# Sliding-window attention and gated layer on one core: where a step's loads, odd value copies and small norm stand in the queues

## The chip, the cores and the metric

The kernel runs on 1 core of one Trainium2 chip. The metric is the device time of one execution in microseconds (us). Four executions of the kernel before took 284.91 to 287.67 us, median 287.3 us. The profiled one took 287.19 us; its span, from the first to the last instruction, is 285.5 us, and its granted TensorE clock is 0.998.

## The reference

Windowed attention on 8 batches, 8 heads, 576 positions, head size 64, and then a two-layer network on the 4608 tokens of 512 features:

```python
scores = (1.0 / np.sqrt(D)) * np.matmul(q, k.transpose(0, 1, 3, 2))
mask = np.abs(pos[:, None] - pos[None, :]) <= 32
attn = softmax(np.where(mask, scores, -1e9))          # rows sum to 1 (+1e-09)
x = np.matmul(attn, v).transpose(0, 2, 1, 3).reshape(B * S, H * D)
h = x @ w_in                                          # 512 -> 2048
g = h * (1.0 / (1.0 + np.exp(-1.702 * h)))
return (g @ w_out).astype(np.float32)                 # 2048 -> 512
```

## The kernel before

Tokens are cut into 36 units of 128 and 18 pairs of 256. The order of work on every engine is written out by hand. `head` and `window(4)` do the first pairs; `steady(w)` runs for w = 5 to 17 and is a software pipeline over three pairs: attention of pair w (units 2w and 2w+1), first layer of pair t = w-1 and second layer of pair o = w-2; `last` and `close` empty the pipeline. Both layers use seven block products in place of eight (`seven` and `product`, on VectorE sums `x_sums`, `g_sums`, and weight sums made once).

The attention of a step: `scores` needs kT and qT (transposed keys and queries in a ring of 1536 tokens); ScalarE takes the exponential, VectorE multiplies the band mask (`band`); `values_two` multiplies with the values, of which two copies are kept: `ve` (8 units, as loaded) and `vo` (the same shifted by 64 tokens, the "odd value copies", made by `odd_pair` with DMAs on SyncE's queue). Heads 0 to 6 of both units go to one pair of banks, head 7 to bank b0; `norm_two(w, 7)` (lines 387, 388) divides head 7, the "small norm", and `norm_two(w, 0)` (lines 390, 391) divides the rest and issues `x_T`: two DMA transposes that make xT of pair w (line 404, SyncE's queue). The first layer of pair w begins in step w+1 and needs that xT; its x sums are line 728.

`seven(t, 1, 0)` writes into bank b0, so TensorE can't start it until the small norm has read it.

Transfers of a step, in the order of their queues before the change:
- GpSimd: `gate` (line 784), a copy of one element of xT[w-1] that can't run until that xT has landed, and then `loads(w)`: two loads into `ve` (units 2w+6, 2w+7), two of k rows and two of q rows (units 2w+8, 2w+9); at a batch boundary one of them is cut in two.
- SyncE: `odd_pair(2w+2)` (lines 190 to 195, two or three copies), xT of pair w (line 404, two transposes), `feed(w)` (line 172, two kT and two qT transposes of units 2w+6 and 2w+7, whose rows `loads(w-1)` brought), and two output stores (line 516). `feed` runs up to w = 14.

Each engine issues its list strictly in order, so an item of SyncE's list that waits holds those behind it. The outputs go through three `o_sb` buffers: in the program, `result(o, 22)` of a step (line 505) waits for the first store of the step before.

In `head`, the q rows of the third tile of 512 tokens are transposed on TensorE into bank "o" four times and copied out by ScalarE; the first second-layer product of `window(4)` (line 436) takes the same bank "o".

Of the kernel before, what the change touches and what calls it, by code (L numbers as in the profile page):

```python
# [27 lines left out]
class _Kernel:  # L28
# [504 lines left out]
    def head(self):  # L533

        nc, dve, act, pool = self.nc, self.nc.vector, self.nc.scalar, self.nc.gpsimd
# [131 lines left out]

        def rows(hp):
            self.rows_T("k", 2, hp, "t", dve)
            self.rows_T("q", 2, hp, "o", act)  # L670

        self.seven(2, 1)
        self.move("side", "main", dve)
# [7 lines left out]
        self.move("k2", "main", act)  # L681
        self.layer1(2, 1, "b")
        rows(0)
        self.x_T(6, "b")
        self.seven(2, 7)
        self.move("k7", "side", act)
        self.seven(2, 5)
        rows(1)
        self.move("22", "main", dve, "k7")
        self.layer1(2, 2, "b")  # L690
        self.gelu(2, "22", 1, 1)
        rows(2)
        self.layer1(2, 3, "b")
        self.seven(2, 4)
# [85 lines left out]
    def steady(self, w):  # L780

        dve, act = self.nc.vector, self.nc.scalar
        a, b, t, o = 2 * w, 2 * w + 1, w - 1, w - 2
        self.nc.gpsimd.tensor_copy(self.gate[0:1], self.xT[t][0:1, 0, 255:256])  # L784
        self.loads(w)
        self.product(o, 1, "o")
        self.scores(a, which=0)
        self.scores(b, which=1)
        if w + 1 < self.NW:
            self.odd_pair(2 * w + 2)  # L790
        self.keep(o, 1, dve)
        self.g_sums(o, 0, (0,))
        self.product(o, 2, "t")
        self.g_sums(o, 0, (1,))
        self.g_sums(o, None, (2,))
        self.product(o, 6)
        self.result(o, 11)
        self.product(o, 5, "t")
        self.keep(o, 6, dve)
        self.band(a)  # L800
        self.seven(t, 1, 1)
        self.product(o, 7)
        self.band(b)
        self.x_sums(t, (0,))
        self.move("side", "main", dve, half=1)
        self.values_two(w)
        self.gelu_table()
        self.x_sums(t, (1,))
        self.keep(o, 7, dve)
        self.seven(t, 2, 1)  # L810
        self.x_sums(t, (2,))
        self.norm_two(w, 7)
        self.seven(t, 6, 1)
        self.gelu(t, "side", 0, 0, 1)
        self.norm_two(w, 0)
        self.seven(t, 1, 0)
        self.move("k2", "main", act, half=1)
        self.product(o, 4)
        self.move("side", "main", dve, half=0)
        self.seven(t, 7, 1)  # L820
        self.x_sums(t, (3,))
        if w == 5:
            self.w_in_sums(0, (2,))
        self.seven(t, 5, 1)
        self.move("k7", "side", act, half=1)
        self.seven(t, 2, 0)
        self.move("22", "main", dve, "k7", 1)
        self.feed(w)
        self.seven(t, 6, 0)
        self.gelu(t, "side", 0, 0, 0)  # L830
        self.seven(t, 4, 1)
        self.g_sums(o, None, (3,))
        self.move("k2", "main", act, half=0)
        self.seven(t, 7, 0)
        self.result(o, 22)
        self.gelu(t, "22", 1, 1, 1)
        self.seven(t, 3, 1)
        self.move("21", "side", dve, "k2", 1)
        self.move("k7", "side", act, half=0)
        self.seven(t, 5, 0)  # L840
        self.gelu(t, "21", 1, 0, 1)
        self.product(o, 3)
        self.move("22", "main", dve, "k7", 0)
        self.result(o, 21, act)
        self.gelu(t, "main", 0, 1, 1)
        self.seven(t, 4, 0)
        self.result(o, 12)
        self.gelu(t, "22", 1, 1, 0)
        self.seven(t, 3, 0)
        self.move("21", "side", dve, "k2", 0)  # L850
        self.gelu(t, "main", 0, 1, 0)
        self.g_sums(t, 1, (0,))
        self.gelu(t, "21", 1, 0, 0)
        self.g_sums(t, 1, (1,))
# [88 lines left out]
    def window(self, w):  # L943

        dve, act = self.nc.vector, self.nc.scalar
        a, b = 2 * w, 2 * w + 1

        def run(lst, n=1):
            for _ in range(min(n, len(lst))):
                lst.pop(0)()  # L950

        l2 = [(lambda u=u, i=i: self.layer2(u, i, "oh"[u % 2], (dve, act)[u % 2])) for u in (4, 5) for i in range(4)]
        run(l2)
        self.scores(7, which=0)
        self.scores(a, which=1)
        run(l2, 2)
        self.band(7)
        self.scores(b, which=0)
        run(l2)
        self.band(a)  # L960
        self.values(7, "th")
        self.gelu_table()
        self.band(b)
        self.norm(7)
        run(l2, 2)
        self.values(a, which=1)
        self.values(b, which=0)
        run(l2)
        self.x_T(7, "t", act)
        self.norm(a)  # L970
        self.x_T(a)
        self.norm(b)
        self.x_T(b)
        run(l2)
        self.loads(w)
        self.odd_pair(10)
        self.w_sums(2, 0)
        self.chain(w - 1, ("b", "a", "b", "a"), lambda: self.feed(w),
                   lambda: [self.w_sums(n, 1) for n in (0, 1, 2, 3)])
        self.g_sums(w - 1, 1, (0, 1))  # L980

    def close(self):
# [91 lines left out]
```

## Time and profile before

| What | Value |
|---|---|
| Profiled execution: its time, its span | 287.19 us, 285.5 us |
| Median of 4 executions (lowest, highest) | 287.3 us (284.91, 287.67) |
| Busy share: PE, DVE, ACT, POOL | 96%, 83%, 73%, 37% |
| Chain that ended last: PE, DMA, DVE, ACT | 41%, 25%, 13%, 10% |
| DMA queue of GpSimd (loads), packets | 97232, 84.6% of 16 engines' span |
| DMA queue of SyncE, packets | 49504, 52.1% |
| xT issues of steps 5 to 17, first and last | 85.87 us, 257.85 us |

The distance between the xT issues of two steps (line 404 in the timeline of SyncE) is a step's length; the twelve distances sum to 171.98 us. The gate's start (line 784 in the timeline of POOL) tells when an xT had landed, since the gate waits for it. A busy PE is not one at its peak, as matmuls are pipelined; so a step's length says more than PE's share. DMA shares of the two queues overlap and can add up to more than 100%.

### The profile page before, as it was taken

The numbers are of one execution on the slowest core, as the hardware profiler recorded it, in microseconds if no ns is written. First come the engines' busy times: TensorE is split into PE (matmuls) and PEld (weight loads), VectorE is DVE, ScalarE is ACT, GpSimd is POOL, SyncE is SP. The second block draws the span as 40 slices with busy tenths as digits, with TensorE's granted clock in tenths as the row PEclk, the third lists the DMA queues.
The fourth block names the chain that finished last, engine by engine and source line by source line (L and its number), as shares of the span: only waits on it lengthen the run. The fifth ranks groups of instructions, "written<-read, shape, count | busy, mean of one in ns | idle before, by whom it ended". The sixth has DMA issues, their size and how long they took to land.

```text
span 285.5 us, 10594 instructions
## 1 busy us (share of the span) xinstructions
PE 274.5 (96%) x4477; PEld 233.2 (82%) x4478; DVE 236.4 (83%) x550; ACT 207.3 (73%) x343; POOL 106.1 (37%) x153
## 2 busy tenths in 40 slices
PE   7999999999999999999999999999989999999995
PEld 2668654865989798989898989898979898989994
DVE  7765567789899889898988888989878989898783
ACT  4576466695778778787887787878777878787360
POOL 8864424997170344434343453433420000000000
PEclk9999999999999999999999999999999999999999
DMA  9999999999999999999999999999999543213022
GB/s 154 188 198 205 200 183 157 175 138 120 207 149 141 131 207 169 166 157 182 137 197 118 215 136 205 161 173 176 146 109 217 137 120 88 66 49 89 27 77 74
DMA packets 147232, 42.42 MB, mean 149 GB/s; under 512 B 130416, under 2 KB 141424, under 8 KB 147184
## 3 DMA queue, kind: packets, MB, share of 16 engines
q0 software_dynamic: 97232, 18.16, 84.6%
q1 hardware_dynamic: 49504, 23.19, 52.1%
q8 instruction: 35, 0.57, 0.9%
q10 hardware_dynamic: 448, 0.39, 0.5%
q14 instruction: 13, 0.11, 0.1%
HBM read 36.96 MB, written 9.44 MB: 163 GB/s over the span
## 4 chain that ended last, share of the span: by engine, by line
PE 41%; DMA 25%; DVE 13%; ACT 10%; POOL 6%; issue 3%; SPq 1%; POOLq 0%; DVEq 0%; ACTq 0%
PE o_ps L487 16%; PE h_main L751 12%; DMA xT<-x 10%; PE h_side L751 9%; DMA w_out_sb<-in_moe_w_out_dram 5%; DMA qs<-in_q_dram 4%; ACT g L768 3%; DMA w_in_sb<-in_moe_w_in_dram 3%; ACT L310 2%; DVE h_side L123 2%; DVE xs L728 2%; DMA ve<-in_v_dram 2%; ACT p L310 2%; POOL ve L177 2%; ACT p L308 2%
## 5 line engine op out<-in xcount | busy, mean ns | idle before, releaser
L751 PEld LDWEIGHTS <-w_in_sb 128*128 128x128 f16 x960 | 59.5, 98 | 7.0 <-issue 2.4
L487 PEld LDWEIGHTS <-gs 128*128 128x128 f16 x480 | 45.3, 98 | 6.0 <-DVE gs L466 0.8
L784 POOL COPY gate<-xT 1x1 f16<-1x1 f16 x13 | 4.0, 310 | 116.0 <-DMA xT<-x 116.0
L751 PEld LDWEIGHTS <-wi_sum 128*128 128x128 f16 x720 | 43.3, 98 | 0.0
L768 ACT ACTIVATE g<-hs 128x512 f16<-128x512 f32 x60 | 37.8, 630 | 0.6 <-DVE hs L763 0.6
L177 POOL DMA_DIRECT2D ve<-in_v_dram x41 | 34.5, 857 | 9.8 <-DMA w_out_sb<-in_moe_w_out_dram 3.5
L751 PE MATMUL h_main<-xs,wi_sum 128*128 128x128 f16 x480 | 36.4, 219 | 0.0
L487 PEld LDWEIGHTS <-g 128*128 128x128 f16 x360 | 32.9, 98 | 3.8
L751 PE MATMUL h_side<-xs,w_in_sb 128*128 128x128 f16 x480 | 34.3, 219 | 0.0
L768 ACT ACTIVATE g<-h_side 128x512 f16<-128x512 f32 x30 | 17.9, 598 | 21.9 <-PE h_side L751 21.6
L763 DVE TENSOR_TENSOR hs<-h_main,hs 128x512 f32<-128x512 f32 x30 | 20.7, 691 | 12.9 <-ACT hs L123 8.4
L487 PE MATMUL o_ps<-w_out_sb,g 128*128 128x256 f16 x240 | 31.1, 273 | 0.0
L487 PE MATMUL o_ps<-w_out_sb,gs 128*128 128x256 f16 x240 | 30.9, 273 | 0.0
L123 ACT COPY hs<-h_side 128x512 f32<-128x512 f32 x30 | 17.5, 583 | 18.1 <-PE h_side L751 17.9
L487 PE MATMUL o_ps<-w_sum,gs 128*128 128x256 f16 x240 | 28.7, 273 | 0.4 <-DVE gs L466 0.4
L436 PE MATMUL o_ps<-w_out_sb,g 128*128 128x512 f16 x96 | 23.4, 380 | 0.7 <-ACT qT L123 0.7
L320 DVE TENSOR_TENSOR p<-p,mask 128x1024 bf16<-128x1024 bf16 x32 | 22.2, 699 | 2.2 <-ACT p L310 0.7
L165 POOL DMA_DIRECT2D qs<-in_q_dram x27 | 23.0, 882 | 2.1 <-DMA ks<-in_k_dram 1.6
L165 POOL DMA_DIRECT2D ks<-in_k_dram x27 | 23.0, 880 | 0.0
L424 PE MATMUL h_ps<-xT,w_in_sb 128*128 128x256 f16 x192 | 22.6, 273 | 0.0
L123 DVE COPY part<-o_ps 128x256 f32<-128x256 f32 x45 | 18.9, 421 | 4.3 <-PE o_ps L487 4.3
L763 DVE TENSOR_TENSOR hs<-h_side,hs 128x512 f32<-128x512 f32 x30 | 20.6, 687 | 1.4 <-PE h_side L751 0.9
(112 smaller groups left out, 546.0 us busy)
## 6 DMA issues: line engine op xcount, KB each, us to landing
out_dram<-o_sb SPq DMA_DIRECT2D x34, 256.0 KB, 4.2
ve<-in_v_dram POOLq DMA_DIRECT2D x31, 128.0 KB, 7.5
ks<-in_k_dram POOLq DMA_DIRECT2D x24, 128.0 KB, 8.1
qs<-in_q_dram POOLq DMA_DIRECT2D x24, 128.0 KB, 10.5
vo<-ve SPq DMA_DIRECT2D x22, 132.0 KB, 6.2
w_in_sb<-in_moe_w_in_dram POOLq DMA_DIRECT2D x4, 512.0 KB, 8.8
w_out_sb<-in_moe_w_out_dram POOLq DMA_DIRECT2D x4, 512.0 KB, 14.4
ve<-in_v_dram POOLq DMA_DIRECT2D x10, 64.0 KB, 5.9
```

Source lines behind the costliest of these rows:

```text
L123: (eng.copy if eng is self.nc.scalar else eng.tensor_copy)(out, in_)
L165: self.nc.gpsimd.dma_start(self.stage[key][off:off + m, n], src[b, :, s:s + m, :].rearrange("h s d -> s h d"))
L177: self.nc.gpsimd.dma_start(self.ve[lo + off:lo + off + n, m % NV, :, :self.D], self.v[b, :, s:s + n, :].rearrange("h s d -> s h d"))
L308: nc.scalar.activation(p[:, eo], sc[eo], AF.Exp, scale=self.scale)
L310: nc.scalar.activation(p.rearrange("k e h s -> k e (h s)"), both, AF.Exp, scale=self.scale)
L320: self.nc.vector.tensor_mul(pv, pv, msk.to_broadcast([128, 8, 2, SQ]))
L424: nc.tensor.matmul(hps[:, i, :], self.w_in_sb[:, kr, ff * 128:(ff + 1) * 128], self.xT[t][:, kr, :], start=(i == 0 and kr == 0), stop=(i = ...
L436: nc.tensor.matmul(o_ps, self.g[t][:, ff, s * 128:(s + 1) * 128], self.w_out_sb[:, ff, :], start=(ff == 0), stop=(ff == self.NFF - 1))
L487: nc.tensor.matmul(self.part[t, key], x, y, start=(first and k == 0), stop=(k == 7), skip_group_check=True)
L751: self.nc.tensor.matmul(dst[:, f], a, b, start=(n in (1, 7) and f == 0 and k == 0), stop=(f == 3 and k == 1), skip_group_check=True)
L763: self.nc.vector.tensor_add(hs[key, half], hs[src, half], hs[add, half])
L768: self.nc.scalar.activation(self.g[t][:, at:at + 4, 128 * v:128 * v + 128], self.hs[src, half], AF.Gelu_apprx_sigmoid)
```

## The change

Four edits. (1) In a steady step, `odd_pair`, the gate and `loads(w)` are put behind `norm_two(w, 0)`, and the gate reads xT[w] in place of xT[w-1]. On SyncE's queue the odd copies of a step come behind its xT; on GpSimd's queue each step's loads wait for that step's xT. (2) `x_sums(t, (2,))` stands behind the small norm on VectorE, not ahead of it. (3) The fourth q copy of the third tile uses a "b" bank. (4) The first g sum of the first steady step is made at the end of `window`.

```diff
@@ head @@
-            self.rows_T("q", 2, hp, "o", act)
+            self.rows_T("q", 2, hp, "ooob"[hp], act)
@@ steady @@
-        self.nc.gpsimd.tensor_copy(self.gate[0:1], self.xT[t][0:1, 0, 255:256])
-        self.loads(w)
         self.product(o, 1, "o")
         self.scores(a, which=0)
         self.scores(b, which=1)
-        if w + 1 < self.NW:
-            self.odd_pair(2 * w + 2)
         self.keep(o, 1, dve)
-        self.g_sums(o, 0, (0,))
+        if w > 5:
+            self.g_sums(o, 0, (0,))
         self.product(o, 2, "t")
...
         self.seven(t, 2, 1)
-        self.x_sums(t, (2,))
         self.norm_two(w, 7)
         self.seven(t, 6, 1)
+        self.x_sums(t, (2,))
         self.gelu(t, "side", 0, 0, 1)
         self.norm_two(w, 0)
+        if w + 1 < self.NW:
+            self.odd_pair(2 * w + 2)
+        self.nc.gpsimd.tensor_copy(self.gate[0:1], self.xT[w][0:1, 0, 255:256])
+        self.loads(w)
         self.seven(t, 1, 0)
@@ window @@
+        self.g_sums(w - 1, 0, (0,))
         self.g_sums(w - 1, 1, (0, 1))
```

No instruction is added or removed but for the place of these. In a steady step SyncE's list becomes: xT of pair w, `odd_pair(2w+2)`, `feed(w)`, two stores.

## The prediction

> **What bounds the kernel now.** I read the windows view first, with one window from xT issue to xT issue (a step), then the chain, the queues' timelines and the waits.
>
> ```profile
> 142.94:157.67 14.73, 14.29 (x251) 12.91 (x249) 12.57 (x29) 11.51 (x19) 5.98 (x9) 1.00 1.97 159
> 186.26:200.29 14.03, 14.02 (x251) 12.72 (x249) 12.48 (x29) 11.51 (x19) 5.14 (x8) 1.00 1.74 179
> 200.29:216.68 16.39, 15.20 (x269) 13.76 (x267) 13.21 (x30) 11.82 (x20) 4.51 (x6) 1.00 1.76 141
> 229.73:243.74 14.01, 14.00 (x251) 12.70 (x249) 12.46 (x29) 11.51 (x19) 0.18 (x1) 1.00 0.30 79
> sum 171.98, PE 168.83 PEld 153.23 DVE 151.46 ACT 137.98 POOL 50.42; mean PE 14.07 PEld 12.77 DVE 12.62 ACT 11.50 POOL 4.20
> ```
>
> Columns: window, length, busy PE, PEld, DVE, ACT, POOL, clock, DMA share, GB/s. The clock is full everywhere. The floor is 14.02 us: a late step almost without DMA (share 0.30) has it, so there the compute engines set the pace. Twelve steps at 14.02 are 168.24; the sum is 171.98, so 3.74 us of waits stand above the floor. The long steps lie where the DMA share is near 2, and the chain shows what ended last in one:
>
> ```profile
> 144.88 9.23 DMA xT<-x
> 154.21 0.29 DVE xs L728
> 155.63 0.20 DVE xs L728
> 155.95 0.30 DVE x L388
> 156.30 0.62 PE h_main L751 x8
> ```
>
> The xT landed at 154.11, 0.6 us after VectorE wanted it. Then VectorE works down to the small norm (L388), and TensorE's next product starts right behind that. The two queues of this step:
>
> ```profile
> 139.50 0.32 POOL L784 COPY gate<-xT 1x1 f16<-1x1 f16 x1 [7.74 <-DMA xT<-x]
> 143.94 1.78 POOL L165 DMA_DIRECT2D qs<-in_q_dram  x2
> 154.24 0.30 POOL L784 COPY gate<-xT 1x1 f16<-1x1 f16 x1 [8.52 <-DMA xT<-x]
> ```
>
> ```profile
> 142.94 3.19 SPq L404 DMA_TRANSPOSE xT<-x  x2
> 146.24 2.64 SPq L172 DMA_TRANSPOSE kT<-ks  x2
> 148.97 5.09 SPq L172 DMA_TRANSPOSE qT<-qs  x2
> 154.17 0.99 SPq L516 DMA_DIRECT2D out_dram<-o_sb  x2
> 155.33 0.47 SPq L190 DMA_DIRECT2D vo<-ve  x1
> ```
>
> Call L the time from an xT issue to the gate that it lets pass. Here it is 154.24 - 142.94 = 11.30 us. In the nine steps from 85.87 it is 11.46, 10.22, 10.79, 10.58, 11.30, 9.55, 9.96, 10.35, 11.83, mean 10.67; in the last gated one (243.74 to 247.59), without loads, 3.85. From a gate to the next xT issue takes 3.44 us when the xT is the late one (139.50 to 142.94), so an xT costs nothing while L stays under 14.02 - 3.44 = 10.6. The steps lie just on that edge. Two more waits matter:
>
> ```profile
> PEld L751 <- DVE x L388: 2.4, 11, 0.3
> PE o_ps L436 <- ACT qT L123: 0.7, 1, 0.7
> ```
>
> **The change, part by part.**
>
> *Small norm ahead of an x sum.* VectorE's place of `x_sums(t, (2,))` costs 0.20 us (155.63 to 155.83) and now comes behind L388. TensorE waited for L388 eleven times, 2.4 us, 0.22 each. Eleven times 0.20 is 2.2 us taken from the floor, which becomes some 13.8. The displaced sum is wanted by the product after next, over 1 us later. Bounds: 0 if another wait holds the step, -2.4.
>
> *First g sum in `window`.* VectorE is idle for 0.50 us at 77.85; the sum (0.34 us of its time) fits there. In the chain VectorE's g sums end at 79.87 and TensorE's product starts at 79.92, so about 0.3 us comes off. Bounds 0 and -0.34.
>
> *q copy in another bank.* It frees TensorE of the 0.7 us above. What hides it: six odd copies on VectorE (60.24 to 64.83) and then a band, for which the values at 65.48 wait whatever TensorE did. I take 0; without that cover it would be -0.7.
>
> *Odd copies behind xT.* Two or three copies (0.5 us of SyncE each, median 6.2 us to landing) no longer stand ahead of xT. In the 16.39 us step xT was ready at 215.4 and issued at 216.68, behind three copies; that goes. They are wanted by `values_two` one step later, about 3 us ahead of the next xT issue, so 11 us after this one. They should land one or two us behind xT, so by L = 8 there is 1 us to spare.
>
> *Loads behind this step's xT.* The gate still passes when an xT lands, so loads start at the same point of a step; but each step's loads come one step later, and one step's worth of transfers vanishes from the crowded time before the first xT (85.87, where loads issued at 78.51 to 83.93 were under way and L was 11.46). So L starts low and creeps up. Its bounds are 3.85 (no loads) and 10.67 (as now). The nearest rows are 5.63 (216.68 to 222.31, two loads) and 8.49 (69.49 to 77.98, loads but no copies ahead). I take 8, nearer the second. Then the late xT costs nothing: the excess of three places goes, 0.75 (the step 85.87 to 100.64), 0.45 (the step to 157.67, less the ring copies that stay) and 1.40 (16.39 + 13.05 less two floors), together 2.6 of the 3.74.
>
> The Trainium skill speaks against that ("DMA: Bandwidth & Descriptors", "Issuing engines are not separate DMA queues"): transfers from all engines share the same 16 DMA engines and interleave, so an order among them makes no bandwidth. The share of 1.97 above agrees that they are crowded. By that rule the 2.6 us would stay, and the sum below would end at 286.4.
>
> *The new wait.* `feed(w)` transposes rows that `loads(w-1)` brought, and those now start only when xT[w-1] has landed. Before, the same rows had been started one step earlier. SyncE stands in order: a kT or qT that waits for its rows holds the two stores, and these the next xT. Let D be the time from gate to the landing of the last qs: 5.3 us to its issue (139.50 to 144.8) and 11.0 to land (median of the stretch 97 to 216), so 16.3; I take the page's 10.5, which makes 15.8, because fewer transposes of SyncE run beside it. Count from X, the issue of the xT ahead of those loads, in steps of 14.0:
> - last qT issue at X + L + D, the first store 1.3 us later, the next xT 2.4 later. That xT wants X + 28.0: no hold while L + D is under 25.6.
> - the first store lands 5.0 us after its issue (median of the same stretch), so X + L + D + 6.3. The sum of the next step that takes an output buffer (L505, at 145.43 where xT was issued at 142.94, so 2.5 behind) waits for it; it wants X + 30.5. No stall while L + D is under 24.2. Behind it VectorE queues the moves for the last gelus, on which exponential, band and next xT hang.
>
> With 8 + 15.8 = 23.8 this just fits. As L creeps up, and with the cut loads at batch boundaries, I charge 1 us over the limit in five steps. A stall of this loop is shared by three steps (first xT, loads, stores, next but one xT), but it can meet each of the three loops; I take a third a step, 1.7 us. Bounds: 0, and rival three.
>
> **Sum**, against the profiled execution of 287.19 (span 285.5 and 1.7 around it; 0.1 under the median of 287.3): -2.2 - 0.3 - 2.6 + 1.7 = -3.4, which makes **283.8 us**.
>
> **Rivals.**
> 1. *No new wait*: loads land well ahead of `feed` and all steps run at the floor of 13.8: -0.3 - 2.2 - 3.7, 281.0. For it: with loads gone from SyncE's crowded stretch D may be 14. Against: the sum of DMA work in a step is the same.
> 2. *The queues stay full*: the DMA engines' work from one xT landing to the next is the same set, so L is back at 10.6 after two steps. The xT stays late, the floor is not reached, and the norm's gain drowns in it: 287.19 - 0.3 and 0.2 for each of the two last steps, 286.5. For it: shares of 1.7 to 1.97 in all steps with loads. Against: the mean step with loads is only 0.3 above the floor.
> 3. *Stores wait for loads* (slower): L + D stays at 10.67 + 16.3 = 27.0. From the store-bound sum to the next xT are 14.0 - 2.5 = 11.5 us, so three steps take L + D + 6.3 + 11.5 = 44.8, 14.93 a step. Nine steps are 134.4 against 130.81 now (85.87 to 216.68): +3.6, less 0.3: 290.5. With 11.83 and 17.2 (the longest rows) 15.6 a step, 296. It decides from L + D = 24.2 on, where my value is 23.8. Against: the first xT has no loads beside it, so the count starts low.
>
> **How the numbers follow.** Forecast 0.43 (its own range 282.3 to 285.5), rival one 0.17, two 0.22, three 0.18. About 1%, 2.9 us, is what a measurement of this kernel can tell from no change. Faster by more (under 284.3): 0.33 of the forecast and all of rival one, 0.50. Slower by more: most of rival three, 0.15. The rest, 0.35, is within. The range goes from a little under rival one, 280.8, to 290.0, into rival three.
>
> **What would show it.** The new gate behind the first steady xT passes 4 to 7 us after that xT's issue (now 11.46), later ones 7 to 9. The wait for L388 falls under 0.5 us. Steps 6 to 10 are 13.8 to 13.9 long. On SyncE, L172 waits for ks and qs in most steps. I am wrong if L is over 10 in the third or fourth step (rival two), or if an o_sb sum of VectorE waits for a store, or xT's issue comes late behind stores, for over 1 us a step (rival three).

## The result, and the profile after

The changed kernel takes 285.69 us (median of 51 runs, 283.31 to 293.43), the kernel before beside it 287.84 us (77 runs, 283.84 to 293.92). The ratio is 0.9962, 95% interval 0.9944 to 0.998. The ratio leaves out runs over 1.5% above the fastest of the same kernel, and the more runs there are, the lower the fastest lies; so here it is nearer to 1 than the ratio of the medians (0.9925), and the experiments below, with fewer runs, are given with both ratios. The gain is 0.4 to 0.7%, where 1.2% was forecast; the prediction gave 0.35 to a change within 1%. The profiled execution took 285.69 us, span 284.0, clock 0.994.

The windows of the changed kernel from xT issue to xT issue (columns as before: length, busy PE, PEld, DVE, ACT, POOL, clock, DMA share, GB/s):

```profile
143.68:157.56 13.88, 13.88 (x251) 12.77 (x249) 12.29 (x29) 11.58 (x19) 6.74 (x9) 1.00 1.86 161
199.29:213.55 14.26, 14.26 (x256) 13.12 (x254) 12.47 (x29) 11.50 (x19) 5.99 (x9) 1.00 1.72 167
213.55:228.10 14.55, 13.36 (x243) 12.18 (x241) 12.67 (x29) 11.53 (x19) 2.90 (x4) 1.00 1.76 164
228.10:242.61 14.51, 14.51 (x259) 13.33 (x257) 12.50 (x29) 11.51 (x19) 0.18 (x1) 1.00 0.63 119
242.61:256.52 13.91, 13.91 (x252) 12.73 (x250) 12.72 (x31) 11.45 (x19) 0.18 (x1) 1.00 0.29 78
sum 168.75, PE 167.12 PEld 153.22 DVE 150.67 ACT 138.04 POOL 55.27; mean PE 13.93 PEld 12.77 DVE 12.56 ACT 11.50 POOL 4.61
```

Eight of the twelve steps now take 13.81 to 13.99 us, with loads too, and the 16.39 us step is gone. The twelve steps lost 3.23 us (171.98 to 168.75). What is left lies late: 14.26, 14.55 and 14.51 us in the ninth to eleventh step, and 14.25 in the second.

The chain of waits of the changed kernel, in two of these (the second step and the tenth):

```profile
96.56 1.29 SPq L172
...
97.96 6.65 DMA out_dram<-o_sb
...
217.99 7.72 DMA vo<-ve
225.71 0.04 issue
225.75 0.64 PE pv L375 x29
```

In the place of `xT<-x` stand a store and an odd copy. The store was issued behind feed's last transpose (L172) and landed 6.65 us later, 0.5 us after the output sum wanted its buffer. The copy of the last step with loads came when `values_two` already stood waiting for it. The waits of the stretch 85 to 260 us (total, times, longest) say the same:

```profile
PE pv L375 <- DMA vo<-ve: 1.4, 2, 1.2
DVE o_sb L505 <- DMA out_dram<-o_sb: 0.7, 2, 0.5
```

The wait for L388 (2.4 us in the kernel before) is not in the list any more, nor one of an x sum for xT.

A step of SyncE's queue and GpSimd's beside it, for the L and D of the prediction (the gate is line 815 now):

```profile
157.56 2.58 SPq L404 DMA_TRANSPOSE xT<-x  x2
160.25 0.53 SPq L190 DMA_DIRECT2D vo<-ve  x1
160.83 0.59 SPq L194 DMA_DIRECT2D vo<-ve  x1
161.52 0.54 SPq L195 DMA_DIRECT2D vo<-ve  x1
162.16 2.52 SPq L172 DMA_TRANSPOSE kT<-ks  x2
164.78 3.20 SPq L172 DMA_TRANSPOSE qT<-qs  x2
168.09 0.99 SPq L516 DMA_DIRECT2D out_dram<-o_sb  x2
171.47 1.50 SPq L404 DMA_TRANSPOSE xT<-x  x1
```

```profile
165.47 0.22 POOL L815 COPY gate<-xT 1x1 f16<-1x1 f16 x1 [8.05 <-DMA xT<-x]
169.47 1.78 POOL L165 DMA_DIRECT2D qs<-in_q_dram  x2
180.04 0.18 POOL L815 COPY gate<-xT 1x1 f16<-1x1 f16 x1 [8.79 <-DMA xT<-x]
```

L is 165.47 - 157.56 = 7.9 here. It was 5.36 behind the first xT and 7.5 to 9.4 in the nine steps whose xT has the loads of a step beside it (mean 8.51). The stores are issued 10.5 us behind xT and 2.6 behind the gate, so beside the loads.

Not all of the profile's difference is the change's. The kernel's first second-layer product (L436, in `head`, well ahead of the four edits), up to which all the kernels here run the same instructions, starts at 34.82 us in this execution and at 31.83 in that of before. Two rows of each (windows view), before and then after:

```profile
18.00:22.00 4.00, 3.38 (x52) 2.85 (x47) 3.28 (x11) 3.09 (x5) 2.58 (x8) 1.00 1.24 206
22.00:26.00 4.00, 4.00 (x39) 3.58 (x37) 1.12 (x2) 2.62 (x6) 1.84 (x7) 1.00 1.24 206
```

```profile
18.00:22.00 4.00, 2.15 (x32) 1.44 (x27) 2.19 (x7) 1.97 (x3) 1.20 (x3) 0.91 1.25 207
22.00:26.00 4.00, 4.00 (x29) 3.14 (x28) 1.85 (x6) 1.78 (x3) 2.98 (x11) 0.67 1.24 206
```

TensorE was idle for 1.85 of 4 us (1.2 us of it in one wait for first-layer weights, `w_in_sb`), and in the 4 us behind that its granted clock was 0.67. The two don't always go together: in the profiles of no_loads and feed_late_four below TensorE was busy for 2.17 and 2.41 us there, waited as long for the weights, kept a clock of 1.00, and L436 started at 33.58 and 33.66 us. By these (an estimate across executions) the wait costs some 1.7 us of the start and the lower clock the rest. The span's difference of 1.5 us is made of +2.99 (start up to L436), -1.10 (from there to the first steady xT: 54.05 to 52.95), -3.23 (twelve steps) and -0.20 (the rest).

### The profile page after: what moved, and what is told of

It is laid out like the page before. It is cut to its first block, busy times and chain, and to the rows that moved or that the text cites. A ratio compares the mean times of both kernels' runs of the same rounds, so it can differ in the third digit from the quotient of the medians.

```text
span 284.0 us, 10588 instructions
## 1 busy us (share of the span) xinstructions
PE 274.0 (96%) x4477; PEld 234.2 (82%) x4478; DVE 233.9 (82%) x550; ACT 207.3 (73%) x343; POOL 105.4 (37%) x153
## 4 chain that ended last, share of the span: by engine, by line
PE 69%; DMA 15%; ACT 5%; SPq 3%; DVE 2%; POOL 2%; issue 1%; POOLq 0%; DVEq 0%
PE o_ps L487 22%; PE h_main L751 14%; PE h_side L751 12%; PE h_ps L424 7%; PE o_ps L436 7%; DMA w_in_sb<-in_moe_w_in_dram 3%; DMA xT<-x 3%; DMA vo<-ve 3%; DMA ks<-in_k_dram 2%; DMA out_dram<-o_sb 2%; PE sc L300 2%; PE pv L375 2%; DMA ve<-in_v_dram 2%; SPq L172 2%; ACT g L768 1%
## 5 line engine op out<-in xcount | busy, mean ns | idle before, releaser
L751 PEld LDWEIGHTS <-w_in_sb 128*128 128x128 f16 x960 | 59.4, 98 | 2.5
L123 ACT COPY hs<-h_side 128x512 f32<-128x512 f32 x30 | 17.5, 583 | 15.7 <-PE h_side L751 15.6
L424 PE MATMUL h_ps<-xT,w_in_sb 128*128 128x256 f16 x192 | 24.1, 283 | 1.2 <-DMA w_in_sb<-in_moe_w_in_dram 1.2
L436 PE MATMUL o_ps<-w_out_sb,g 128*128 128x512 f16 x96 | 23.4, 380 | 0.0
L424 PEld LDWEIGHTS <-w_in_sb 128*128 128x128 f16 x192 | 19.0, 101 | 4.0 <-DMA w_in_sb<-in_moe_w_in_dram 1.4
## 6 DMA issues: line engine op xcount, KB each, us to landing
w_out_sb<-in_moe_w_out_dram POOLq DMA_DIRECT2D x4, 512.0 KB, 14.2
```

The lines of the kernel that those rows point to most:

```text
L123: (eng.copy if eng is self.nc.scalar else eng.tensor_copy)(out, in_)
L424: nc.tensor.matmul(hps[:, i, :], self.w_in_sb[:, kr, ff * 128:(ff + 1) * 128], self.xT[t][:, kr, :], start=(i == 0 and kr == 0), stop=(i = ...
L436: nc.tensor.matmul(o_ps, self.g[t][:, ff, s * 128:(s + 1) * 128], self.w_out_sb[:, ff, :], start=(ff == 0), stop=(ff == self.NFF - 1))
L751: self.nc.tensor.matmul(dst[:, f], a, b, start=(n in (1, 7) and f == 0 and k == 0), stop=(f == 3 and k == 1), skip_group_check=True)
```

## Experiments

All but after_again and before_again (one execution each) were timed beside the kernel before on the same chip. "Sum" is that of the twelve steps in the profiled execution; "loads land" is the time from a gate to the landing of the last q load behind it (mean of the steps where the trace has it); L is the mean of the nine steps whose xT has a step's loads beside it.

| Kernel | Ratio to before [95%] | Ratio of medians | Sum | L | Loads land |
|---|---|---|---|---|---|
| changed | 0.9962 [0.9944, 0.998] | 0.9925 | 168.75 | 8.51 | 14.2 |
| norm_only | 0.996 [0.9903, 1.0016] | 0.9979 | 172.62 | 10.74 | 15.8 |
| copies_only | 0.9967 [0.9923, 1.001] | 0.9922 | 169.96 | 9.11 | 14.8 |
| loads_only | 1.0137 [1.0059, 1.0215] | 1.0132 | 173.83 | 8.09 | 13.2 |
| starts_only | 1.0018 [0.9978, 1.0057] | 1.0010 | 175.26 | 9.92 | 18.7 |
| no_loads | 0.9859 [0.9807, 0.9911] | 0.9859 | 168.95 | 9.19 | 15.0 |
| no_norm | 0.9943 [0.9903, 0.9984] | 0.9940 | 170.25 | 7.70 | 13.3 |
| feed_only | 0.9916 [0.9872, 0.996] | 0.9857 | 169.37 | 8.85 | 13.8 |
| four_outputs | 0.9954 [0.9905, 1.0003] | 0.9940 | 174.21 | 10.06 | 15.6 |
| feed_half | 0.993 [0.9878, 0.9982] | 0.9889 | 168.62 | 8.70 | 14.1 |
| feed_late | 0.9806 [0.9757, 0.9854] | 0.9789 | 166.38 | 7.30 | 12.7 |
| feed_late_four | 0.9798 [0.9729, 0.9868] | 0.9728 | 166.28 | 6.94 | 12.5 |
| no_loads_feed | 0.9857 [0.9785, 0.9928] | 0.9808 | 172.25 | 8.87 | 15.5 |
| no_stores | 0.9806 [0.974, 0.9873] | 0.9744 | 166.35 | 5.73 | 12.5 |
| no_feed | 0.9817 [0.975, 0.9883] | 0.9744 | 166.40 | 4.11 | 10.5 |

The kernel before has L of 10.67 and 10.20 and loads that land after 16.7 and 14.8 us in its two profiles.

### Each part alone

**norm_only**: edit (2) on the kernel before.

```diff
-        self.x_sums(t, (2,))
         self.norm_two(w, 7)
         self.seven(t, 6, 1)
+        self.x_sums(t, (2,))
```

> The kernel before with the second edit alone (the x sum behind the small norm). Theory A (the gain lies in the twelve steady steps and the terms add up): the wait for L388 falls from 2.4 us to under 0.5, the steps that the xT does not hold go from 14.02 to 13.8, but the three held ones stay, so the twelve steps take 170.0 to 170.5 us in place of 171.98; time -1.6 us, ratio 0.994. Theory B (what the profile of before showed above the floor is not typical of its runs, so only the norm counts): all of the measured gain, ratio 0.996.

Measured 0.996 [0.9903, 1.0016]. In the profiled execution (290.36 us, above the median of 287.44) early steps were 13.84 to 13.92, so the floor falls by 0.18 us (from 14.02 to 13.84). Then L grew from 9.6 to 12.9 and steps of 14.98, 16.33 and 15.71 came. Its waits from 85 to 260 us:

```profile
DVE xs L728 <- DMA xT<-x: 3.6, 3, 1.8
```

So the floor's gain can be lost again to a late xT. That the shorter steps make xT late isn't shown: this is one profile of a long execution, starts_only has steps of up to 15.72 us in another such execution without this edit, and the interval of the ratio holds the value of either theory.

**copies_only**: `odd_pair` behind `norm_two(w, 0)`, and nothing else.

```diff
-        if w + 1 < self.NW:
-            self.odd_pair(2 * w + 2)
         self.keep(o, 1, dve)
...
         self.norm_two(w, 0)
+        if w + 1 < self.NW:
+            self.odd_pair(2 * w + 2)
```

> The kernel before with the odd copies alone put behind the xT of their step; loads and gate stay. Theory A: two or three copies fewer stand ahead of each xT, so the mean time from xT issue to gate falls from 10.7 us to 9 and the late steps lose most of their 3.7 us; ratio 0.992 to 0.994. Theory B, and rival two of the prediction (the set of transfers between two xT is the same, so the xT lands no earlier): ratio 1.000, L stays at 10 to 11.

Measured 0.9967 [0.9923, 1.001]; steps of 14.02 to 14.16 but for 14.39 and 14.9, no x sum waits for xT, and the wait for L388 stays (1.5 us). L is 9.1, which is theory A's number. In this profile the edit takes the late xT away by itself; the interval of the ratio holds the values of both theories.

**loads_only**: gate and `loads(w)` behind `norm_two(w, 0)`, copies left ahead of xT.

```diff
-        self.nc.gpsimd.tensor_copy(self.gate[0:1], self.xT[t][0:1, 0, 255:256])
-        self.loads(w)
         self.product(o, 1, "o")
...
         self.norm_two(w, 0)
+        self.nc.gpsimd.tensor_copy(self.gate[0:1], self.xT[w][0:1, 0, 255:256])
+        self.loads(w)
```

> The kernel before with the gate and the loads alone put behind this step's xT; the odd copies stay ahead. Theory A: the first xT lands 4 to 7 us after its issue, later ones after 8 to 9; no late xT, twelve steps in 169 to 170 us, ratio 0.992; the copies of a step land well ahead of their use, so no product waits for them. Theory B: ratio 0.998 to 1.000. Rival three of the prediction (stores wait for the loads): ratio over 1.005, with o_sb sums of VectorE waiting for stores.

Measured 1.0137 [1.0059, 1.0215], slower, by a wait that neither theory had. SyncE's own waits (stretch 97 to 226 us):

```profile
SPq L192 <- DMA ve<-in_v_dram: 13.0, 6, 4.2
SPq L195 <- DMA ve<-in_v_dram: 3.4, 2, 2.1
```

The odd copies need values that are now loaded one step later, and ahead of xT they hold the queue: xT was issued 3.4 to 4.7 us after it was ready in five steps, and 2.6 in a sixth. The ratio is rival three's, but its wait isn't there: output sums waited 0.4 us for a store, once. So edit (1) is one edit of two halves; the loads can't be moved without the copies.

**starts_only**: edits (3) and (4).

```diff
-            self.rows_T("q", 2, hp, "o", act)
+            self.rows_T("q", 2, hp, "ooob"[hp], act)
...
+        self.g_sums(w - 1, 0, (0,))
         self.g_sums(w - 1, 1, (0, 1))
```

> The kernel before with the third and fourth edits alone (another bank for one q copy; the first g sum in the window stage). Both theories: the first steady xT 0.3 to 0.7 us earlier counted from the first second-layer product, nothing after it; ratio 0.998 to 0.999.

Measured 1.0018 [0.9978, 1.0057]: nothing that can be seen. From L436 to the first steady xT it took 52.91 us, where the kernel before took 54.05 and, in before_again, 53.32; the kernels without these edits took 53.2 to 53.5. With all profiles of this document, the twelve kernels that have both edits took 52.91 to 53.37 us (median 53.0) and the six that don't 53.23 to 54.05 (median 53.4). So some 0.4 us is gained there, too little to be seen in the time.

### One part out, and feed behind the stores

**no_loads**: all but the loads' half of edit (1).

```diff
+        self.nc.gpsimd.tensor_copy(self.gate[0:1], self.xT[t][0:1, 0, 255:256])
+        self.loads(w)
         self.product(o, 1, "o")
...
-        self.nc.gpsimd.tensor_copy(self.gate[0:1], self.xT[w][0:1, 0, 255:256])
-        self.loads(w)
```

> All edits but one: gate and loads stay at the head of the step and read xT of the pair before; copies behind xT, norm ahead of the x sum and both start edits are made. Theory A now says: the copies ahead of xT were what made xT late, and the norm's floor of 13.85 counts only once xT is in time. Copies alone had L of 9.0 to 10.2, and the limit is 10.4 with the shorter floor; so L stays under 10.4, ten of the twelve steps are 13.8 to 14.1, the twelve sum to 167 to 168.5, and the ratio to the kernel before is 0.988 to 0.994, no worse than with the loads moved (0.996). Rival C: shorter steps leave the queues less time, as with the norm alone, where L grew from 9.6 to 12.9 and three steps were 15 to 16.3; then L passes 11 in the middle steps, the sum is 169.5 to 171.5 and the ratio 0.995 to 1.0: the loads' move is needed to keep xT in time.

Measured 0.9859 [0.9807, 0.9911], which doesn't touch the changed kernel's interval: the loads' move, which the prediction gave the gain to, costs 0.7% (by the medians) to 1%. The sum of its one profile (168.95) is no lower than that of the changed kernel's, so the place of the loss isn't seen there. Rival C falls: L stays under 11.

**no_norm**: the changed kernel without edit (2).

```diff
+        self.x_sums(t, (2,))
         self.norm_two(w, 7)
         self.seven(t, 6, 1)
-        self.x_sums(t, (2,))
```

> The changed kernel with one edit undone: the x sum stands ahead of the small norm again. Theory A: the loads and copies keep xT in time (L 7 to 9.5), so the norm's wait alone sets the steps: they are 14.02 to 14.1 in place of 13.8 to 13.95, the wait of a weight load for L388 is back (about 1.5 to 2.4 us over the run), the steps sum to about 170.5 (168.75 and 12 x 0.17 less what the late steps hide) and the ratio to the kernel before is 0.999 to 1.004. Rival D: in the changed kernel other waits (copies for the values, stores for the output sums) end the steps, and the norm's gain is hidden: sum 168.5 to 169.3, ratio within 0.002 of the changed kernel's 0.996.

Both were half right. The steps are those of theory A (14.01 to 14.12, one of 15.64 in which an output sum waited 1.7 us for a store; the L388 wait of 2.4 us is back), the ratio is rival D's: 0.9943 [0.9903, 0.9984], which can't be told from that with the norm (by the medians 0.9940 and 0.9925). With longer steps the loads land in 13.3 us, L is 7.7 (8.51 and 8.71 in the two profiles of the changed kernel), and no value waits for a copy. This fits that the waits which eat the norm's gain are those that its shorter steps bring; it rests on one profile.

**feed_late**: the changed kernel, with feed behind the stores on SyncE's queue.

```diff
-        self.feed(w)
         self.seven(t, 6, 0)
...
         self.result(o, 12)
+        self.feed(w)
         self.gelu(t, "22", 1, 1, 0)
```

> The changed kernel with one more edit: on SyncE's queue feed(w) stands behind the two stores of the step. Theory A: the new wait that the prediction charged with 1.7 us is a store behind feed; with the stores first the wait of an output sum for a store goes, step 6 (14.25) falls to 13.9 and the sum of the twelve steps to about 168.2; the ratio to the kernel before falls by 0.001 to 0.002 to 0.994 to 0.995. Steps 14 to 16 (14.27, 14.55, 14.50) stay if their cause is the copies that arrive behind the values, as the wait of the values product for vo says. Rival E: kT and qT now land later and the scores wait for them: steps 14.0 to 14.4 and the ratio 0.998 to 1.003.

Measured 0.9806 [0.9757, 0.9854], 282.18 us, far more than either theory had, and all six runs lie between 281.77 and 282.87. Every step has the floor, the late ones too:

```profile
155.52:169.36 13.84, 13.84 (x250) 12.54 (x247) 12.62 (x31) 11.51 (x19) 5.43 (x7) 1.00 1.94 174
210.99:224.83 13.84, 13.84 (x252) 12.71 (x250) 12.48 (x29) 11.51 (x19) 2.35 (x4) 1.00 1.78 180
224.83:238.67 13.84, 13.84 (x252) 12.72 (x250) 12.48 (x29) 11.51 (x19) 0.18 (x1) 1.00 0.31 81
sum 166.38, PE 166.38 PEld 152.57 DVE 150.26 ACT 138.26 POOL 54.88; mean PE 13.87 PEld 12.71 DVE 12.52 ACT 11.52 POOL 4.57
```

Its queue in the step that was shown of the changed kernel:

```profile
155.52 3.29 SPq L404 DMA_TRANSPOSE xT<-x  x2
...
160.84 0.99 SPq L516 DMA_DIRECT2D out_dram<-o_sb  x2
161.93 3.14 SPq L172 DMA_TRANSPOSE kT<-ks  x2
165.16 2.62 SPq L172 DMA_TRANSPOSE qT<-qs  x2
```

The stores go 5.3 us behind xT and ahead of the gate (162.55). The last odd copy lands 8.3 us behind xT's issue on average and 9.3 at most (changed kernel: 9.7 and 10.6 over steps 5 to 13, 12.2 in the step behind), and neither the values nor an output sum waits for a transfer.

**after_again**: the changed kernel in one more execution.

> The changed kernel once more, for one look at how its start scatters. Theory A: the twelve steps sum to 168.0 to 169.5 again and the last part is 27.4, while the first second-layer product of the start lies anywhere from 31.8 to 35.2 us, since the start up to there is the same code in all kernels and showed these values. Rival F: the changed kernel's steps themselves scatter as those of the unchanged queues did (172.0 to 175.3), so 168.75 was a lucky profile and this one is over 170.

Rival F was right. The start was near that of the kernel before (32.25 us to L436), the twelve steps took 171.17 us, with 14.93, 15.10, 15.60 and 14.51 among them, and the time was 285.94 us, nearly that of the first. Output sums waited 2.2 us for stores, the values 2.4 for copies. So the profile above had 2.4 us fewer waits in its steps, and a late start that hid it.

### Which wait, or the transfers as a whole

**four_outputs**: the changed kernel with four output buffers; xT gives one up to make room.

```diff
-... name="xT", tag="xT", bufs=4)
+... name="xT", tag="xT", bufs=3)
-... name="o_sb", tag="o_sb", bufs=3)
+... name="o_sb", tag="o_sb", bufs=4)
```

> The changed kernel with four buffers for the outputs in place of three (and three in place of four for xT, whose fourth isn't in use); the queues are as changed. Theory A: the new wait is an output sum (L505) that waits for a store behind feed. With a fourth buffer that wait is gone (0.7 and 2.2 us in two profiles of the changed kernel, and 15.1 in place of 13.84 in a step that has it), steps 6, 7 and 12 are 13.8 to 13.95, steps 14 to 16 stay long (14.3 to 15.6, the values wait for copies), the twelve sum to 167.5 to 169.5 and the ratio to the kernel before is 0.984 to 0.991. Rival G: the stores' place helped because feed's transposes no longer ran beside the loads and copies, and the output buffer had little to do with it; then the ratio stays at 0.993 to 0.998 with waits for vo or for kT in more steps.

Theory A, that the output sum's wait is the cause, falls: 0.9954 [0.9905, 1.0003], with no wait of an output sum for a store left. Others are there in its place (85 to 260 us of the profiled execution, which at 289.11 us is above the median of 286.85):

```profile
PE pv L375 <- DMA vo<-ve: 5.7, 7, 1.3
PEld L375 <- DMA vo<-ve: 5.5, 6, 1.4
DVE xs L728 <- DMA xT<-x: 0.3, 1, 0.3
```

L grew to 10.7, the loads landed 15.6 us behind their gate, and the copies were late. A likely reason, not shown, is that without the stall for a buffer the queues have less time to catch up; the profile is one of a long execution.

**feed_only**: the kernel before, with feed behind the stores (the same diff as feed_late's).

> The kernel before with one edit: feed(w) behind the two stores; copies and loads stand ahead as before. In the kernel before no output sum waits for a store, and the waits are three late xT and the small norm. Theory A: feed's place matters only where copies and feed stand between xT and the stores, so nothing is gained: the L388 wait and late xT stay, steps sum to 171 to 175, ratio 0.996 to 1.002. Rival H: feed right behind xT is what crowds the DMA engines in every order of the queues, and moving it helps here as much as in the changed kernel: sum 168.5 to 170, ratio 0.983 to 0.99.

By the ratio between the two, 0.9916 [0.9872, 0.996]; the sum (169.37) is rival H's. Ten of its twelve steps are 14.01 to 14.07, one 14.11, the first 14.97; no x sum waits for xT, and only the L388 wait is left (1.8 us). So feed's place, which the prediction didn't question, counts in the old order too: this one edit, on the kernel before, is worth no less than the four edits together (by the medians 0.9857, and 0.9925 for the changed kernel).

**no_loads_feed**: no_loads with feed behind the stores.

> The changed kernel with the loads' move undone and feed(w) behind the stores: copies behind xT, norm ahead of the x sum, both start edits. Theory A: with copies and feed out of the way the loads' place has little to do; xT has L of 8 to 9.5, all steps 13.8 to 14.0, sum 166.4 to 167.5, ratio 0.979 to 0.984, as the same with loads moved (0.9806, sum 166.4). Rival I: loads started a step earlier still run beside the copies and xT (waits for vo of 1.7 us without feed's move): sum 168 to 169 and ratio 0.985 to 0.99, so the loads' move is worth 0.5% once the stores go first.

0.9857 [0.9785, 0.9928]; runs from 281.36 to 287.03, and the profiled one (287.03) had 16.46 and 15.85 among its early steps and 13.84 to 13.95 in the last seven. The intervals of this and feed_late overlap: what the loads' move is worth once feed stands last isn't settled.

**before_again**: the kernel before in one more execution.

> The kernel before once more, for one look at its steps. Theory A: the profile of before had a low sum for its kind of queues; this one has 172 to 175.5 (starts_only 175.3 with the same queues), so that the changed kernel's own scatter (168.8 and 171.2) is against a like scatter of before. Rival F: 172.0 is what before does, within 0.5.

170.66 us in twelve steps (285.29 us), lower than the first profile, so neither holds: the kernel before scatters by more than 0.5 in both directions (starts_only, with the same queues, had 175.26 in an execution of 289.93 us).

### Taking work out of the queues

**no_stores**: the changed kernel without the stores of ten steps (their outputs stay unwritten).

```diff
         if t == self.NW - 1:
             self.store(u, cols)
+        elif 3 <= t < 13:
+            pass
         elif n in (12, 22) and s == 0 or n == 21:
```

> The changed kernel without the two stores of the steps that have a feed (ten steps: their outputs are left out). In the changed kernel the last q load of a step lands 13.5 to 15.8 us behind its gate, mean about 14, with feed behind the stores 11.8 to 12.8 in the later steps; a step needs 13.84. Theory A2: the transfers of a step all but fill it, and it is the stores standing behind feed, so running beside the loads, that make the loads land late (stores take 6 to 7 us there, 3 us when they go ahead of the gate). Without stores the loads land 11 to 12.8 us behind the gate, L is 6 to 8, all steps 13.84 to 13.95, ratio 0.976 to 0.983. Rival J: feed's four transposes right behind xT and the copies are what delays these and with them the gate; the stores matter little: L stays at 8 to 10, waits for vo stay, ratio 0.988 to 0.995.

**no_feed**: the changed kernel without feed's transposes in ten steps (`feed(w, "")` issues none; old kT and qT are used).

```diff
-        self.feed(w)
+        self.feed(w, "")
         self.seven(t, 6, 0)
```

> The changed kernel without the four kT and qT transposes of the ten steps (scores then use old rows of the ring). The stores then stand right behind the copies. Both theories expect less work in the queues and all steps at 13.84 to 13.95, ratio 0.976 to 0.982; they differ in the loads: by A2 the loads gain only by the stores' earlier place and land 11.5 to 12.8 us behind the gate, as with feed behind the stores, and L is 6 to 7.5; by J xT and copies are freed of the transposes beside them and L falls to 4 to 5.5.

0.9806 [0.974, 0.9873] and 0.9817 [0.975, 0.9883]: each brings all steps to 13.82 to 13.94 and ends every wait for a transfer on the compute engines. Without stores the loads land in 12.5 us and L is 5.7, as A2 had it (L even lower). Without feed the loads land in 10.5 us and L is that of an xT alone, which is J's number. The xT of one step and the gate it lets pass (timelines of SyncE and of GpSimd, no_feed):

```profile
154.57 2.52 SPq L404 DMA_TRANSPOSE xT<-x  x2
```

```profile
158.44 0.18 POOL L815 COPY gate<-xT 1x1 f16<-1x1 f16 x1 [7.72 <-DMA xT<-x]
```

3.87 us, where an xT without loads in the kernel before took 3.84 to 3.91. On average the loads land 10.5 us behind their gate and the next xT is issued 10 us behind it, so it has hardly any load beside it. So neither theory alone: two stores weigh 1.7 us of the loads' landing and four transposes 3.7, and to leave out either is enough to end the waits.

**feed_half**: the changed kernel with the kT transposes ahead of the stores and the qT transposes behind.

```diff
-        self.feed(w)
+        self.feed(w, "k")
...
+        self.feed(w, "q")
```

> The changed kernel with half of feed, the two qT transposes, behind the stores, and the two kT ahead. The stores are then issued some 2.6 us earlier than in the changed kernel, about 8 us behind xT's issue, close to the gate. Theory A2: what counts is whether the stores are under way before the loads; half of them would be, so loads land 13 to 14 us behind the gate and the ratio lies between 0.981 and 0.996, at 0.984 to 0.991. Rival J: two transposes stay right behind the copies and two go; the same middle value. If the ratio is that of feed fully behind (0.978 to 0.983), the last transposes, which wait for q rows, are what held the stores. Rival K: the gain of feed_late was a luck of its six runs; then 0.993 to 0.998 here too.

0.993 [0.9878, 0.9982], less than half of the gain. The stores are issued 0.5 us ahead of the gate on average (changed kernel 2.6 behind it, feed_late 2.4 ahead), the loads land in 14.1 us, and the values wait 2.2 us for copies. Rival K can't be excluded by this ratio; feed_late_four excludes it.

**feed_late_four**: feed_late with the buffers of four_outputs.

> Feed behind the stores, with four output buffers and three for xT: a control for the run with four output buffers, which was no faster than the changed kernel. Theory A2: no output sum waits for a store here in any case, and a fourth xT buffer isn't in use, so steps of 13.84 to 13.95, sum 166.3 to 166.8, ratio 0.978 to 0.983. Rival L: three xT buffers or the moved addresses cost something by themselves, and hid the gain of the fourth output buffer: then 0.985 to 0.995 here.

0.9798 [0.9729, 0.9868]: the time of feed_late again (281.28 us, 280.61 to 282.69). With the stores first, four output buffers and three for xT cost nothing; that they cost nothing in four_outputs, with feed first, isn't shown by it. And with the stores first the fourth output buffer has nothing to do. It is the fastest version here, though not apart from feed_late.

## Why the prediction was wrong, point by point

- **What bounds the kernel**: right. The late xT and the small norm set the steps; each went when its edit was made (copies_only, norm_only). But its size was read off one execution: before_again has 2.4 us over a floor of 14.02 a step, where the first profile has 3.74.
- **Small norm**: -2.2 us was right for the floor (14.02 to 13.84 a step), and the bound "0 if another wait holds the step" is what it brought to the time: no_norm (0.9943) can't be told from the changed kernel. The step that failed is the adding of this gain to waits that were held fixed: the prediction kept L at 8 and the copies at nothing whatever the step. Without the norm the compute engines waited 1.7 us for transfers (85 to 260 us), with it 2.4 and 4.6.
- **Late xT**: half right in mechanism. L fell from 10.67 to 8.51, and no x sum waited for xT. But the copies' place is enough for that, and the loads' isn't needed: copies_only shows the first, loads_only (1.0137) and no_loads (0.9859) show what the second costs. And the 2.6 us were read off one execution: in before_again the three largest excesses over the floor come to 2.1. The prediction named the wait for rows on SyncE (feed), and missed the one of the copies for `ve`, since in the changed order xT is ahead of them.
- **Copies**: "by L = 8 there is 1 us to spare" was the thinnest step and was costed at nothing. L came to 9.4 and the copies of the last loaded step, in three pieces, landed 12.2 us behind xT's issue (13.2 in after_again): 1.4 and 0.3 us of waiting values, 1.9 and 0.5 in after_again, and the two steps around it were 1.4 and 2.4 us over two floors of 13.84.
- **The new wait**: it is there, at L505 as named, but by another route. The prediction let the stores wait for rows (L + D, with D = 15.8). D is 14.2, and 8.5 + 14.2 = 22.7 is under its limit of 24.2; SyncE's waits for qs were 4.0 us in all. What holds the stores is SyncE's own issuing: eight or nine transfers ahead of them, so they go 10.6 us behind xT; issued behind the gate they take 5.4 us on average and up to 7.1, and the sum wants the buffer 16.1 to 16.4 us behind xT. The mean just fits and the longest don't: 0.7 and 2.2 us in the two profiles. That this is near the 1.7 charged is luck, as the route was another. Nor is the wait the change's alone: in starts_only, whose queues are as before, output sums waited 2.2 us for stores. And taking this wait away (four_outputs) gains nothing.
- **So the term that was mis-sized** is what is left over the floor: 1.7 us for the stores and nothing for the copies. By the prediction the twelve steps should come to 171.98 - 2.2 - 2.6 + 1.7 = 168.9. The profiled execution has 168.75, after_again 171.17, and feed_late, without these waits, 166.4: they cost 2.4 and 4.8 us, where 2.5 were allowed. The first fits the forecast by luck; it also had a start 3 us late, and both took nearly the same time. From the kernel before to the changed one, the mean of two profiles each falls by 1.4 us in the twelve steps (171.3 to 170.0), where 3.1 were forecast.
- **What stands behind these waits** is in part argued. The step's transfers need as long as the step (loads land 14.2 us behind a gate that comes every 13.84), and whichever transfer is wanted first is the wait that is seen; the prediction counted the waits one by one, each against its own limit. For it: in feed_late, feed_late_four, no_stores and no_feed (10.5 to 12.7 us against 13.84) and in feed_only (13.8 against 14.02) TensorE, VectorE and ScalarE never wait for a transfer from 85 to 260 us; in the changed kernel, feed_half and four_outputs (14.1 to 15.6) they wait 2.2 to 11.5 us. Against it as a rule: no_norm has 13.3 against 14.02 and still a wait of 1.7 us, copies_only has 14.8 and waits of only 0.9 us, and no_loads, at 15.0, is faster than the changed kernel.
- **The Trainium skill** says ("DMA: Bandwidth & Descriptors", "Issuing engines are not separate DMA queues") that DMAs of all issuing engines run on the same 16 DMA engines and interleave. That the order of transfers therefore brings no time is the prediction's reading of it, which would have left 286.4. That was near in number (285.69), but not by its mechanism: no x sum waited for xT. And it doesn't hold: feed_late issues the same transfers in another order and gains 1.4 to 1.6% on the changed kernel. The sharing itself agrees with the runs: with work left out, the loads land 1.7 us (no_stores) and 3.7 us (no_feed) sooner.
- **Rivals**: one (281.0, no new wait) is near what feed_late measured, 282.18, but not the changed kernel. Two had the right kind of cause, queues that stay full and drown the norm's gain, and a wrong L (10.6) and a late xT that didn't come. What was held against it, a mean step with loads only 0.3 us above the floor, leaves out the step of 16.39; with it the nine steps from 85.87 are 0.5 above. Three did not come: no step was held by stores for over 1 us a step throughout.
- **First g sum and bank**: -0.3 and 0 can't be told in the time. In the profiles the stretch from L436 to the first steady xT is some 0.4 us shorter with the two edits, so the size was about right.

What stays open: why the same transfers land their loads 1.5 us sooner with the stores ahead of the gate (14.2 and 12.7 us). In feed_half the stores go only 0.5 us ahead of the gate on average, and the loads land in 14.1; what in the DMA engines makes the difference the traces don't say.

## What to carry to other kernels

When several waits for transfers stand close to their limits, don't cost them one by one: measure how long the transfers of a step take from their release to the last landing, and compare that with the step. Where it is no shorter, expect that a faster step or a wait removed can turn into the next wait, and try less work in the queue, or the transfers that a buffer waits for issued first. Here that one reordering, put on the changed kernel, was worth more (1.4 to 1.6%) than its four edits (0.4 to 0.7%). Take one more profile of the same kernel before a forecast of 1% is built on the waits of one.

## What was not expected of the hardware

- With feed ahead of the stores the changed kernel took 283.31 to 293.43 us from run to run (51 runs); with feed behind them 281.77 to 282.87 (six runs), and 280.61 to 282.69 with four output buffers (six runs). Feed's place alone doesn't do it: no_loads_feed took 281.36 to 287.03 (six runs).
- In the profiled execution of the changed kernel TensorE had 1.85 us of idle time at 18 to 22 us, and a granted clock of 0.67 in the 4 us behind it; the start, of the same code, was 3 us longer. norm_only had the same (1.62 us idle, 0.58, L436 at 35.20 us). no_loads and feed_late_four had as much idle time (1.83 and 1.59 us) and a clock of 1.00, before_again and after_again 0.62 us and 1.00. What decides it the profiles don't show.
